# A retention and gated-FFN kernel on one core: the seven-product px stage gets one attention excursion, loads in halves and a later store; the last block another order of loads

## The chip, the cores and the metric

The kernel runs on one core of one Trainium2 chip. The metric is the device time of one execution in microseconds (us); less is better. The kernel before takes 1502.32 us, the median of three runs (1500.96 to 1503.14).

## The reference

Three stages, all in float32. Retention over 8 sequences of 576 tokens with 8 heads of 64, then two feed-forward stages on the 4608 x 512 result:

```python
scores = scale * np.matmul(q, k.transpose(0, 1, 3, 2))
ret = scores * Dmat[None, :, :, :]          # gamma ** (i - j), causal
x = np.matmul(ret, v)                       # -> 4608 x 512
h = (x @ w1) * (x @ w2) @ w3                # 1024 wide
x2 = h @ w_out                              # 512 wide
h2 = x2 @ w_in
g = h2 * np.clip(h2 + 3.0, 0.0, 6.0) / 6.0  # 2048 wide
out = g @ w_out2
```

## The kernel before, in words

Every float32 matrix product is made from two fp32r parts of each operand, high and low, as three matmuls (high x low, high x high, low x high): the helper `mm3` at lines 130 to 132. Casting the high part is ScalarE's (ACT) work, subtracting it to get the low part VectorE's (DVE; the helper at line 135). The engine names in the rows are PE (TensorE), DVE, ACT, POOL (GpSimd) and SP (SyncE, which here only issues loads).

The weights w3 and w_out are multiplied into one 1024 x 512 matrix first (`Wps`, line 513), kept as `Wh` and `Wl` and written to DRAM as `wsd` by `w_quads`. From then on the 4608 tokens go through nine blocks (j = 0 to 8) of 512 tokens. A block (`ffn1`) has two parts:

- 64 steps of x @ w1 and x @ w2 (`f_a`, `f_b`). Each f gives a bank `pa`, copied out by ACT (line 644), and a bank `pb`, multiplied with it on DVE. Four PSUM banks are used in turn.
- px, the product with the joined matrix, 32 steps. In blocks 0 and 8 it is done whole (`mm3`). In blocks 1 to 7 it is `px_str`: a Strassen-Winograd scheme of seven products of quarter size, 24 matmuls of 128x256 each (line 771, 168 in a px). Each product streams an operand of 1 MB (`wb` from `wsd`, `load_w`, line 728) into one of three buffers. Operands 0 and 1 are loaded during the first part, operand 2 when px starts; operand i + 3 goes into the buffer of operand i when product i has ended. Products use banks A, C, B, D, A, D, C: the sixth product adds to bank D, after DVE has read the fourth out of it (line 746, `x<-px`), and the seventh to bank C.

The order of the work is written out by hand: `at(s, f)` puts a piece of work into step s, and every `mm3` and some matmuls of px call `tick`, which emits what stands in that step. `B0 + SPB * n` is the first step of block n, with SPB = 96; `E0` is the first step of block 8. Each engine and each DMA queue then runs its own instructions in the order in which they were emitted, so a wait at the head of one holds up all that is behind it. SP, which has no other work, issues loads as soon as their own waits allow, however early that is in steps.

Between the matmuls stand four attention excursions a block (`excursion`, table `ex`): small matmuls for one tile of 128 tokens (lines 214, 251), after which DVE makes P, S and x (lines 228, 247, 289) and loads of `kv` and `qk` two tiles ahead are issued from POOL (lines 198, 193). `v_scale` (line 204) scales a loaded kv tile on DVE.

Also between them, the weights of the second feed-forward are prepared, one "i" job (w_in) and one "q" job (w_out2) a block (`job`): two raw loads of 512 KB (`wr`), `weights` on ACT (lines 155, 156) and DVE (160, 164), sums (859), high part (862), low part (135), and a store of 1.75 MB (870), all through one staging buffer `stg`/`stghi`. Four `w_job`s do the same for the joined matrix in block 0 and 1 (`wj`, lines 592 to 606).

In block 8, `w_again` loads `Wl` and `Wh` back, `load_xop` and `load_set` load the operands of the second feed-forward (`xop`, `wset`).

Of the kernel before, what the change touches and what calls it, by code (L numbers as in the profile page):

```python
# [7 lines left out]
F32 = mybir.dt.float32  # L8
# [19 lines left out]
def retention_moe_kernel(  # L28
# [20 lines left out]
    nc = tc.nc  # L49
# [15 lines left out]
    TPB = BLK1 // 128  # L65
# [7 lines left out]
    NSET = M2 // 2  # L73
# [44 lines left out]
    def at(s, f):  # L118
        slots.setdefault(max(s, now[0]), []).append(f)
# [200 lines left out]
    with tc.manual_schedule():  # L320
# [38 lines left out]
        B0 = LEAD + 8 * KF  # L359
# [112 lines left out]

        ex = {-1: LEAD + 35, 0: LEAD + 40, 1: LEAD + 45, 2: LEAD + 50, 3: LEAD + 55, 4: B0 + 53, 5: B0 + 63, 6: B0 + 74, 7: B0 + 85}
        for t in range(2 * TPB, NTI):
            ex[t] = B0 + SPB * (t // TPB - 1) + (24, 45, 68, 85)[t % TPB]
        for t in range(-1, NTI):
            at(ex[t], lambda t=t: excursion(t))
            if t >= 0:
                if t == TPB - 1:
                    at(ex[t] + 1, lambda t=t: x_out(t))  # L480
                if t + 1 < NTI:
                    at(ex[t] + 1, lambda t=t: (p_mask(t + 1), s_add(t + 1)))
                if t < 3:
                    at(ex[t] + 1, lambda t=t: v_scale(t + 2))
                if t != TPB - 1:
                    at(ex[t] + 1, lambda t=t: x_out(t))
                at(ex[t] + 2, lambda t=t: x_hi(t))
                at(ex[t] + (3 if t < 2 * TPB else 4), lambda t=t: x_lo(t))
                for i in ([4] if t == 1 else [t + 2] if 2 < t < NTI - 2 else []):
                    at(ex[t] + 1, lambda i=i: load_kv(i))  # L490
                for i in ([t + 3] if t + 3 < 2 * TPB else [t + 2] if 2 * TPB <= t + 2 < NTI else []):
                    at(ex[t] + 1, lambda i=i: load_qk(i))
            if 2 < t < NTI - 2:
                at(B0 + 30 if t == 3 else ex[t + 1] - (4 if t < 7 else 5), lambda t=t: v_scale(t + 2))
        at(LEAD + 33, lambda: v_scale(0))
        at(ex[-1] + 1, lambda: (p_mask(0), s_add(0)))
        at(LEAD + 37, lambda: v_scale(1))
# [76 lines left out]
        def w_again(low):  # L574
            if low:
                lo = [Wp.tile([128, n, DM], F32R, tag=t, name=t) for t, n in (("Wl", 5), ("Wm", 3))]
                whole[1] = lambda f: lo[0][:, f] if f < 5 else lo[1][:, f - 5]
            else:
                h = Wp.tile([128, KF, DM], F32R, tag="Wh", name="Wh")
                whole[0] = lambda f: h[:, f]  # L580
            for o, (c, k) in enumerate(quads):
                src = wsd[o].rearrange("k p h n -> p h k n")
                for to, x in ([(h[:, k:k + 4], src[:, 0])] if not low else [(lo[0][:, 0:4], src[:, 1])] if not k else [(lo[0][:, 4:5], src[:, 1, 0:1]), (lo[1], src[:, 1, 1:4])]):
                    nc.gpsimd.dma_start(out=to[:, :, c:c + 256].bitcast(F32), in_=x)

        def w_job(q, s):
            def sums():
# [21 lines left out]
                at(s + d, f)  # L609

        at(B0 + 44, w_quads)
        for q, d in enumerate((65, 73, 81, 92)):
            w_job(q, B0 + d)
        at(B0 + SPB + 1, open_a)
        at(B0 + SPB + 6, open_st)
# [107 lines left out]
        WORD = (0, 4, 5, 6, 1, 3, 7)  # L723
        w_at = {}

        def load_w(i, b):
            w_at[i] = t = st["wb"][:, b] if b < 2 else st["w3"]
            nc.sync.dma_start(out=t.rearrange("p k h n -> p k (h n)").bitcast(F32), in_=wsd[WORD[i]].rearrange("k p h n -> p k (h n)"))

        def px_str(j):  # L730
            e = j % 2
            rt = x_ps[e].tile([128, 4, BLK1], F32, tag="xh", name="x1")
            st["w3"] = x_ps[e].tile([128, 4, 2, 256], F32R, tag="xl", name="wb")
            a, c, b, d = turn
            bank = {k: mm_bank("px", i) for k, i in (("A", a), ("C", c), ("B", b), ("D", d))}
            turn[:] = [a, b, d, c]
            pair, keep = st["pair"], st["keep"]
            load_w(2, 2)

            def two(k):  # L740
                return bank[k].rearrange("p (m n) -> p m n", m=2)

            U, C11, V, W = (rt[:, 0:2, 0:256], rt[:, 0:2, 256:512], rt[:, 2:4, 0:256], rt[:, 2:4, 256:512])

            def add(out_ap, x, y):
                nc.vector.tensor_tensor(out=out_ap, in0=x, in1=y, op=ALU.add)

            def parts(q):
                at(now[0] + q, lambda: nc.scalar.copy(out=pair[q][:, 0, 0:2], in_=keep[q]))
                at(now[0] + q + 2, lambda: sub(nc.vector, pair[q][:, 1, 0:2], keep[q], pair[q][:, 0, 0:2]))  # L750

            after = (lambda: nc.scalar.copy(out=V, in_=two("A")),
                     lambda: [parts(q) for q in range(4)],
                     lambda: add(U, V, two("B")),
                     lambda: (add(W, U, two("D")), add(V, W, two("C"))),
                     lambda: nc.scalar.copy(out=C11, in_=two("A")),
                     lambda: add(W, U, two("D")),
                     lambda: add(U, U, two("C")))
            seen = set()
            for i, (k, o) in enumerate((("A", 0), ("C", 1), ("B", 3), ("D", 4), ("A", 2), ("D", 1), ("C", 0))):  # L760
                w = w_at.pop(i)
                for kk in range(4):
                    for m in range(2):
                        n = 8 * i + 2 * kk + m
                        if 4 * n % 7 < 4:
                            tick()
                        ms = slice(128 * m, 128 * m + 128)
                        out_ap = bank[k][:, 256 * m:256 * m + 256]
                        hi, lo = pair[kk][:, 0, o], pair[kk][:, 1, o]
                        for x, y in ((0, hi), (0, lo), (1, hi)):  # L770
                            nc.tensor.matmul(out=out_ap, lhsT=w[:, kk, x, ms], rhs=y, start=k not in seen, stop=kk == 3 and x == 1, skip_group_check=True)  # L771
                            seen.add(k)
                if i + 3 < 7:
                    load_w(i + 3, (e, 1 - e, 2)[i % 3])
                if i == 1:
                    after[1]()
                else:
                    at(now[0], after[i])
            xs = x_ps[e].tile([128, 2, 4, 256], F32, tag="xl", name="xs")
            hl = [st["wb"][:, i].rearrange("p k h n -> p (k h) n") for i in range(2)]  # L780
            for m, s in enumerate((now[0], now[0] + 14)):
                b1, b2, d = rt[:, m], rt[:, 2 + m], xs[:, m]
                b11, b12, b21, b22 = b1[:, 0:HB1], b1[:, HB1:BLK1], b2[:, 0:HB1], b2[:, HB1:BLK1]
                parts_ = ((0, 2, b2.rearrange("p (o n) -> p o n", o=2)), (6, 7, b1[:, 0:HB1].rearrange("p (o n) -> p o n", o=1)), (2, 6, d))

                def sums(d=d, v=(b11, b12, b21, b22)):
                    for o, a, b in ((0, v[1], v[0]), (1, v[3], d[:, 0]), (2, v[3], v[1]), (3, v[2], d[:, 1])):
                        sub(nc.vector, d[:, o], a, b)

                def hi(parts_=parts_):  # L790
                    for a, b, t in parts_:
                        nc.scalar.copy(out=hl[0][:, a:b], in_=t)

                def lo(parts_=parts_):
                    for a, b, t in parts_:
                        sub(nc.vector, hl[1][:, a:b], t, hl[0][:, a:b])

                def store(m=m):
                    sb = next(i for i, (b0, n) in enumerate(SBS) if b0 <= j < b0 + n)
                    a = HB1 * (j - SBS[sb][0])  # L800
                    for h, t in enumerate(hl):
                        nc.scalar.dma_start(out=xod[sb][:, :, m, h, a:a + HB1].rearrange("o p n -> p o n"), in_=t[:, 0:7].bitcast(F32))

                for x, f in ((1, sums), (2, hi), (3, lo), (6, store)):
                    at(s + x, f)
# [47 lines left out]
        def job(key, srcs, sums_of, outs, s):  # L853
# [15 lines left out]
                    o = outs(hl)  # L869
                    nc.scalar.dma_start(out=o, in_=t if len(o.shape) == 2 else t.rearrange("p (o n) -> p o n", o=7))  # L870

            for d, f in ((10, sums), (11, hi), (14, lo), (19, store)):
                at(s + d, f)

        A_SUMS = ((4, 0, 1, ALU.add), (5, 4, 2, ALU.subtract), (6, 2, 0, ALU.subtract), (7, 3, 5, ALU.subtract))
        B_SUMS = ((4, 0, 1, ALU.subtract), (5, 2, 4, ALU.subtract), (6, 2, 0, ALU.subtract), (7, 3, 5, ALU.subtract))
        for n in range(NSET):
            job(("i", n), (w_in2[n + NSET], w_in2[n]), A_SUMS, lambda hl, n=n: wid[n, hl], B0 + SPB * n + SPB + (20 if n < NSET - 1 else 24))
            job(("q", n), (w_out2[n], w_out2[n + NSET]), B_SUMS,
                lambda hl, n=n: wqd[:, :, n, hl].rearrange("o p n -> p o n"), B0 + SPB * n + SPB + (46 if n < NSET - 1 else 48))  # L880

        wset, xop = {}, {}
        SETS = (0, 1, 2, 3, 4, 5, 6, 7)
# [48 lines left out]
            signs[:] = [xo_p.tile([128, 4 * BLK1], I32, tag="xl", name="raw")[:, 1024:1536]]  # L932
            nc.gpsimd.memset(signs[0], 0)

        at(E0 + 23, late_sign)
        at(E0 + 14, open_late)
        for i, s in enumerate((24, 58, 26, 28, 32, 38, 104)):
            at(E0 + s, lambda i=i: load_xop(0, i))
        WTAGS = ("A1", "B1", "A2", "B2")
        for n, (t, s) in enumerate((("A1", 62), ("B1", 70), ("A2", 80), ("s4", 105), ("s5", 107), ("B2", 112), ("s6", 119), ("s7", 133))):  # L940
# [434 lines left out]
```

## Time and profile before

| | us |
|---|---|
| median of three runs | 1502.32 |
| the profiled execution | 1500.72 |
| its span, first to last instruction | 1499.0 |
| PE busy | 1434.6 (96% of the span) |
| DVE busy | 1091.4 (73%) |
| ACT busy | 572.0 (38%) |
| granted TensorE clock, mean | 0.981 |

The profiled execution lies 1.6 us under the median of the runs; 1.7 us of it lie around the span. PE is the engine that is nearly always busy, so what a change is worth is looked for in the few places where PE waits, and in the stretches where its granted clock is under 1.00 (full speed, 2.4 GHz; 0.50 is 1.2 GHz). A busy PE at half clock is busy for twice as long.

### The profile page before, as it was taken

To read this page: it belongs to the slowest core of one execution; us is meant where nothing else is said; L and a number is where in the kernel's file an instruction comes from. 1 tells how busy PE (TensorE), PEld (TensorE's weight loads), DVE (VectorE), ACT (ScalarE), POOL (GpSimd) and SP (SyncE) were. 2 spreads that over 40 slices of the span, in tenths; PEclk is the share of its full clock that TensorE was granted. 3 is DMA by queue.
4 is the path that set the end of the run, shared out by engine and by line. 5 is a ranking of instruction groups with operands and counts; after the bars stand their busy time and mean duration, and the time that the engine had idled before them with its cause. 6 is when DMAs were issued, how large, how long until landed. Compare 5 with 4: busy or idle time off the path is not lost.

```text
span 1499.0 us, 27907 instructions
## 1 busy us (share of the span) xinstructions
PE 1434.6 (96%) x11315; PEld 1217.8 (81%) x11315; DVE 1091.4 (73%) x1880; ACT 572.0 (38%) x842; POOL 150.1 (10%) x339
## 2 busy tenths in 40 slices
PE   9999889899898989899969999999999999999999
PEld 5588778788787888888857898888888888888888
DVE  7889677858585858586525666666668988988987
ACT  7572333333232424233323343333334333344342
POOL 1101000000000000000101233222221000000000
PEclk9999989999999999999989999999999999999999
DMA  9775776767678678776778975464798444444442
GB/s 364 276 253 175 262 254 238 274 236 273 249 261 292 240 275 288 270 264 246 251 310 312 369 257 196 166 250 165 293 357 304 141 141 141 141 135 132 127 134 65
DMA packets 210801, 351.31 MB, mean 234 GB/s; under 512 B 10384, under 2 KB 139184, under 8 KB 207088
## 3 DMA queue, kind: packets, MB, share of 16 engines
q1 hardware_dynamic: 137392, 208.69, 40.5%
q0 software_dynamic: 22976, 77.91, 14.0%
q10 hardware_dynamic: 50304, 62.92, 12.4%
q8 instruction: 89, 1.46, 0.4%
q14 instruction: 40, 0.33, 0.1%
HBM read 231.51 MB, written 117.96 MB: 233 GB/s over the span
## 4 chain that ended last, share of the span: by engine, by line
PE 86%; DMA 9%; DVE 3%; issue 1%; POOL 0%; ACT 0%; SPq 0%; ACTq 0%; DVEq 0%; POOLq 0%
PE pb L1297 15%; PE pb L130 11%; PE pb L131 11%; PE pb L132 11%; PE pb L1298 8%; PE px L771 8%; DMA wb<-wsd 5%; PE pa L130 4%; PE pa L131 4%; PE pa L132 4%; PE Wps L513 4%; PE z L251 2%; PE sc L214 2%; DMA xop<-xod 1%; DMA wqd<-stg 1%
## 5 line engine op out<-in xcount | busy, mean ns | idle before, releaser
L1297 PE MATMUL pb<-wq,op 128*128 128x512 f32 x1000 | 346.7, 391 | 0.0
L1298 PE MATMUL pb<-wq,op 128*128 128x256 f32 x1000 | 280.0, 280 | 0.0
L1297 PEld LDWEIGHTS pb<-wq,op 128*128 128x128 f32 x1000 | 187.0, 187 | 41.0
L130 PE MATMUL pb<-xop,wset 128*128 128x512 f32 (+1 forms) x558 | 205.9, 369 | 3.1 <-DMA xop<-xod 1.7
L131 PE MATMUL pb<-xop,wset 128*128 128x512 f32 (+1 forms) x558 | 205.3, 368 | 0.0
L132 PE MATMUL pb<-xop,wset 128*128 128x512 f32 (+1 forms) x558 | 205.2, 368 | 0.0
L1175 ACT CAST op<-unit 128x1024 fp32r<-128x1024 f32 x126 | 131.5, 1052 | 174.1 <-DVE unit L1161 146.7
L771 PE MATMUL px<-pair,wb 128*128 128x256 f32 x1176 | 162.0, 301 | 36.6 <-DMA wb<-wsd 35.6
L771 PEld LDWEIGHTS px<-pair,wb 128*128 128x128 f32 x1176 | 157.1, 209 | 39.9 <-issue 36.8
L1298 PEld LDWEIGHTS pb<-wq,op 128*128 128x128 f32 x1000 | 189.0, 189 | 0.0
L135 DVE TENSOR_TENSOR op<-unit,op 128x1024 fp32r<-128x1024 f32 x126 | 154.0, 1223 | 30.9 <-ACT op L1175 30.9
L130 PEld LDWEIGHTS pb<-xop,wset 128*128 128x128 f32 x558 | 105.2, 189 | 22.5 <-issue 2.1
L132 PEld LDWEIGHTS pb<-xop,wset 128*128 128x128 f32 x558 | 105.2, 189 | 17.3
L131 PEld LDWEIGHTS pb<-xop,wset 128*128 128x128 f32 x558 | 105.2, 189 | 17.3
L130 PE MATMUL pb<-xh,w2h 128*128 128x512 f32 x288 | 113.7, 395 | 4.9 <-ACT stg L819 4.9
L131 PE MATMUL pb<-xl,w2h 128*128 128x512 f32 x288 | 112.8, 392 | 0.0
L132 PE MATMUL pb<-xh,w2l 128*128 128x512 f32 x288 | 112.8, 392 | 0.0
L130 PE MATMUL pa<-xh,w1h 128*128 128x512 f32 x280 | 109.8, 392 | 0.0
L131 PE MATMUL pa<-xl,w1h 128*128 128x512 f32 x280 | 109.2, 390 | 0.1
L132 PE MATMUL pa<-xh,w1l 128*128 128x512 f32 x280 | 109.0, 389 | 0.0
L1161 DVE TENSOR_TENSOR unit<-unit 128x1024 f32<-128x1024 f32 x72 | 87.9, 1220 | 0.6
L297 ACT CAST xh<-x 128x512 fp32r<-128x512 f32 x36 | 22.2, 616 | 166.5 <-DVE x L289 166.5
(207 smaller groups left out, 2259.7 us busy)
## 6 DMA issues: line engine op xcount, KB each, us to landing
wb<-wsd SPq DMA_DIRECT2D x49, 1024.0 KB, 9.2
unit<-gd SPq DMA_DIRECT2D x72, 512.0 KB, 5.3
xop<-xod SPq DMA_DIRECT2D x28, 1024.0 KB, 6.1
xod<-wb ACTq DMA_DIRECT2D x28, 896.0 KB, 4.7
qk<-in_qk_dram POOLq DMA_DIRECT2D x36, 512.0 KB, 6.5
kv<-in_kv_dram POOLq DMA_DIRECT2D x32, 512.0 KB, 5.4
gd<-gw POOLq DMA_DIRECT2D x60, 256.0 KB, 3.1
gd<-g POOLq DMA_DIRECT2D x57, 256.0 KB, 4.2
```

The costliest lines, as they stand in the source:

```text
L130: nc.tensor.matmul(out=out_ap, lhsT=sh, rhs=mh, start=first, stop=False, **kw)
L131: nc.tensor.matmul(out=out_ap, lhsT=sh, rhs=ml, start=False, stop=False, **kw)
L132: nc.tensor.matmul(out=out_ap, lhsT=sl, rhs=mh, start=False, stop=last, **kw)
L135: eng.tensor_tensor(out=out_ap, in0=x, in1=y, op=ALU.subtract)
L214: nc.tensor.matmul(out=out_ap, lhsT=lhsT, rhs=rhs, start=True, stop=True, skip_group_check=True)
L251: c["last"] = nc.tensor.matmul(out=out_ap, lhsT=lhsT, rhs=rhs, start=(a, g) not in c["opened"], stop=True, skip_group_check=True)
L513: nc.tensor.matmul(out=ps, lhsT=w3f[:, n // 4 % 8, n % 4 * 128:n % 4 * 128 + 128], rhs=wo[:, j, :], start=j == 0, stop=j == KF - 1)
L771: nc.tensor.matmul(out=out_ap, lhsT=w[:, kk, x, ms], rhs=y, start=k not in seen, stop=kk == 3 and x == 1, skip_group_check=True)
L1161: nc.vector.tensor_tensor(out=f32_unit(o), in0=t[0], in1=t[1], op=f)
L1175: nc.scalar.copy(out=op_tiles(7 * b + p)[0], in_=src())
L1297: nc.tensor.matmul(out=c[k], lhsT=h[:, ts], rhs=w, start=first and kt == 0, stop=False, skip_group_check=True)
L1298: nc.tensor.matmul(out=c[k][:, 0:256], lhsT=l[:, ts], rhs=w[:, 0:256], start=False, stop=kt == 7, skip_group_check=True)
```

## The change

Five edits, all in the hand-written order and in one load helper.

1. The excursions of blocks 1 to 7 stand at steps 24, 39, 54 and 72 of a block, where they stood at 24, 45, 68 and 85. Px is steps 64 to 95, so it holds one excursion in place of two. The kv and qk loads behind the excursion at 72 are issued 19 steps later than the excursion's other work, at step 92.
2. The q job of a block starts at step 70 in place of 46, and its store comes 24 steps after that (step 94) in place of 19 (step 65).
3. `load_w` loads an operand of px in two halves of 512 KB; in px the first half of operand i + 3 is issued when the first half of product i has ended.
4. The third and fourth `w_job` move from steps 81 and 92 of block 0 to 98 and 106, into block 1.
5. In block 8 `w_again` issues from SP in place of POOL, the i job starts at step 12 in place of 24, the q job at 32 in place of 48, and `late_sign`, `open_late` and the first loads of `xop` move by two to ten steps.

```diff
-            ex[t] = B0 + SPB * (t // TPB - 1) + (24, 45, 68, 85)[t % TPB]
+            ex[t] = B0 + SPB * (t // TPB - 1) + (24, 39, 54, 72)[t % TPB]
...
+                late = 19 if t >= 2 * TPB and t % TPB == 3 else 0
-                    at(ex[t] + 1, lambda i=i: load_kv(i))
+                    at(ex[t] + 1 + late, lambda i=i: load_kv(i))
-                    at(ex[t] + 1, lambda i=i: load_qk(i))
+                    at(ex[t] + 1 + late, lambda i=i: load_qk(i))
-                at(B0 + 30 if t == 3 else ex[t + 1] - (4 if t < 7 else 5), lambda t=t: v_scale(t + 2))
+                at(B0 + 30 if t == 3 else ex[t + 1] - 4, lambda t=t: v_scale(t + 2))
...
-                    nc.gpsimd.dma_start(out=to[:, :, c:c + 256].bitcast(F32), in_=x)
+                    nc.sync.dma_start(out=to[:, :, c:c + 256].bitcast(F32), in_=x)
...
-        for q, d in enumerate((65, 73, 81, 92)):
+        for q, d in enumerate((65, 73, 98, 106)):
...
-        def load_w(i, b):
+        def load_w(i, b, halves=(0, 2)):
             w_at[i] = t = st["wb"][:, b] if b < 2 else st["w3"]
-            nc.sync.dma_start(out=t.rearrange("p k h n -> p k (h n)").bitcast(F32), in_=wsd[WORD[i]].rearrange("k p h n -> p k (h n)"))
+            for k in halves:
+                nc.sync.dma_start(out=t[:, k:k + 2].rearrange("p k h n -> p k (h n)").bitcast(F32), in_=wsd[WORD[i], k:k + 2].rearrange("k p h n -> p k (h n)"))
...
-                if i + 3 < 7:
-                    load_w(i + 3, (e, 1 - e, 2)[i % 3])
+                    if kk % 2 and i + 3 < 7:
+                        load_w(i + 3, (e, 1 - e, 2)[i % 3], (kk - 1,))
...
-            for d, f in ((10, sums), (11, hi), (14, lo), (19, store)):
+            for d, f in ((10, sums), (11, hi), (14, lo), (24 if key[0] == "q" and key[1] < NSET - 1 else 19, store)):
...
-            job(("i", n), ... (20 if n < NSET - 1 else 24))
+            job(("i", n), ... (20 if n < NSET - 1 else 12))
-            job(("q", n), ... (46 if n < NSET - 1 else 48))
+            job(("q", n), ... (70 if n < NSET - 1 else 32))
...
-        at(E0 + 23, late_sign)
-        at(E0 + 14, open_late)
-        for i, s in enumerate((24, 58, 26, 28, 32, 38, 104)):
+        at(E0 + 21, late_sign)
+        at(E0 + 24, open_late)
+        for i, s in enumerate((27, 58, 28, 29, 32, 38, 104)):
```

How the instructions stand, at three places.

PE, the px of block 3 and what borders on it; `z` and `sc` are the excursion's matmuls. Before:

```order
L132 MATMUL pb<-xh,w2l 128x512
L771 MATMUL px<-pair,wb 128x256 x21
L251 MATMUL z<-qk,S 64x64 x8
L251 MATMUL z<-P,kv 64x64 x8
L214 MATMUL sc<-qk 64x64 x16
L214 MATMUL sc<-kv 64x64 x16
L251 MATMUL z<-P,kv 64x64 x8
L771 MATMUL px<-pair,wb 128x256 x90
L251 MATMUL z<-qk,S 64x64 x16
L251 MATMUL z<-P,kv 64x64 x8
```

Now:

```order
L132 MATMUL pb<-xh,w2l 128x512
L773 MATMUL px<-pair,wb 128x256 x42
L251 MATMUL z<-qk,S 64x64 x16
L251 MATMUL z<-P,kv 64x64 x8
L214 MATMUL sc<-qk 64x64 x16
L214 MATMUL sc<-kv 64x64 x16
L251 MATMUL z<-P,kv 64x64 x8
L773 MATMUL px<-pair,wb 128x256 x126
```

The only excursion left in px stands behind 42 matmuls, and 126 follow without a break.

DVE, the same px, from the excursion's x (line 289) on. `x<-x,px` (746, now 748) reads a bank of px; 160 and 164 are the q job's weights, `stg<-stg` of line 859 (now 861) its sums, `pair<-keep` px's own operands. Before:

```order
L289 SCALAR_TENSOR_TENSOR x_3945<-z,cw,ut 128x128 x4
L135 TENSOR_TENSOR xl<-x_3945,xh 128x4x128
L135 TENSOR_TENSOR pair<-keep,pair 128x512 x4
L746 TENSOR_TENSOR x_3839<-x_3839,px 128x2x256
L204 TENSOR_TENSOR kv<-kv,rate 128x2x256
L746 TENSOR_TENSOR x_3839<-x_3839,px 128x2x256 x2
```

Now:

```order
L289 SCALAR_TENSOR_TENSOR x_4055<-z,cw,ut 128x128 x4
L160 SCALAR_TENSOR_TENSOR stg<-stg,sign 128x512
L164 SCALAR_TENSOR_TENSOR stg<-wr,stg 128x512
L135 TENSOR_TENSOR pair<-keep,pair 128x512
L135 TENSOR_TENSOR xl<-x_4055,xh 128x4x128
L135 TENSOR_TENSOR pair<-keep,pair 128x512
L160 SCALAR_TENSOR_TENSOR stg<-stg,sign 128x512
L164 SCALAR_TENSOR_TENSOR stg<-wr,stg 128x512
L135 TENSOR_TENSOR pair<-keep,pair 128x512 x2
L748 TENSOR_TENSOR x_3914<-x_3914,px 128x2x256
L861 TENSOR_TENSOR stg<-stg 128x256 x4
L748 TENSOR_TENSOR x_3914<-x_3914,px 128x2x256 x2
```

The q job's four weight operations and its sums now stand ahead of the second and third reading of px's banks.

SP, the loads from the end of block 7's px into block 8. Before:

```order
L728 DMA wb<-wsd 128x4x512 x5
L107 DMA wr<-in_w_in_dram 128x512 x2
L923 DMA xop<-xod_66 128x2048 x4
L107 DMA wr<-in_w_out_dram 128x512
L923 DMA xop<-xod_66 128x2048
L107 DMA wr<-in_w_out_dram 128x512
L923 DMA xop<-xod_66 128x2048
```

Now:

```order
L730 DMA wb<-wsd 128x2x512 x10
L107 DMA wr<-in_w_in_dram 128x512
L585 DMA Wl<-wsd 128x4x256
L585 DMA Wl<-wsd 128x256
L585 DMA Wm<-wsd 128x3x256
L585 DMA Wl<-wsd 128x4x256
L585 DMA Wl<-wsd 128x256
L585 DMA Wm<-wsd 128x3x256
L107 DMA wr<-in_w_in_dram 128x512
L107 DMA wr<-in_w_out_dram 128x512 x2
L585 DMA Wh<-wsd 128x4x256 x4
L925 DMA xop<-xod_66 128x2048 x6
```

The q job's two raw loads stand ahead of all `xop` loads; the `Wl` loads stand ahead of the i job's second raw load.

## Rows read from the trace of the kernel before

**Rows 1.** Waits of PE, whole span: who waited for what, us in total, times, longest.

```profile
PE px L771 <- DMA wb<-wsd: 35.6, 10, 6.4
PE px L130 <- ACT a L644: 13.7, 1, 13.7
PE pb L130 <- ACT stg L819: 4.9, 1, 4.9
```

**Rows 2.** Timeline of PE, px of block 3: start, length, work, [idle before <-releaser].

```profile
381.26 7.39 PE L771 MATMUL px<-pair,wb 128*128 128x256 f32 x39 [4.99 <-DMA wb<-wsd]
...
390.61 7.10 PE L771 MATMUL px<-pair,wb 128*128 128x256 f32 x57
```

**Rows 3.** Stretches around block 3's wait: us, busy (instructions) per engine, PEclk, DMA share, GB/s.

```profile
376.00:379.00 3.00, 0.27 (x3) 0.07 (x1) 2.45 (x5) 0.20 (x1) 0.00 (x0) 1.00 1.03 407
...
381.30:385.00 3.70, 3.70 (x17) 3.70 (x18) 0.00 (x0) 0.00 (x0) 0.00 (x0) 0.50 0.89 334
```

**Rows 4.** DMA issues, 355 to 402 us: KB each, median us to landing; then qk, 160 to 700.

```profile
wb<-wsd SPq DMA_DIRECT2D x5, 1024.0 KB, 10.1
kv<-in_kv_dram POOLq DMA_DIRECT2D x2, 512.0 KB, 7.5
...
wqd<-stg ACTq DMA_DIRECT2D x1, 896.0 KB, 14.0
...
DMA to landing us min/median/max: 4.6/6.8/10.2
```

**Rows 5.** Timeline of PE, px of blocks 1, 2 and 7.

```profile
220.33 7.62 PE L771 MATMUL px<-pair,wb 128*128 128x256 f32 x39 [6.38 <-DMA wb<-wsd]
...
294.25 3.11 PE L771 MATMUL px<-pair,wb 128*128 128x256 f32 x24 [1.46 <-DMA wb<-wsd]
...
699.76 6.39 PE L771 MATMUL px<-pair,wb 128*128 128x256 f32 x39 [3.11 <-DMA wb<-wsd]
```

**Rows 6.** Timeline of ACT: the end of block 0's px, and block 8's q job.

```profile
160.77 0.59 ACT L819 COPY stg<-px 128x512 f32<-128x512 f32 x1 [8.70 <-DMA xod<-stg]
...
766.58 0.66 ACT L155 ACTIVATE stg<-wr 128x512 f32<-128x512 f32 x1 [21.14 <-DMA wr<-in_w_out_dram]
```

**Rows 7.** DMA issues, 714 to 760 us (block 8).

```profile
wid<-stg ACTq DMA_DIRECT2D x1, 896.0 KB, 7.9
```

**Rows 8.** Timeline of PE, block 3's first part: an excursion, then a step.

```profile
349.44 0.69 PE L251 MATMUL z<-qk,S 64*64 64x64 f32 x32
...
351.46 0.50 PE L130 MATMUL pb<-xh,w2h 128*128 128x512 f32 x1
351.80 0.39 PE L131 MATMUL pb<-xl,w2h 128*128 128x512 f32 x1
352.03 0.40 PE L132 MATMUL pb<-xh,w2l 128*128 128x512 f32 x1
```

**Rows 9.** Timeline of DVE, block 3, 349 to 378 us.

```profile
351.60 0.69 DVE L228 TENSOR_TENSOR P<-sc,mask 128x512 f32<-128x512 f32 x1 [2.60 <-PE z L251]
...
360.06 0.69 DVE L164 SCALAR_TENSOR_TENSOR stg<-wr,stg 128x512 int32<-128x512 int32 x1
360.79 1.55 DVE L859 TENSOR_TENSOR stg<-stg 128x256 f32<-128x256 f32 x4
...
370.95 0.69 DVE L228 TENSOR_TENSOR P<-sc,mask 128x512 f32<-128x512 f32 x1
371.56 0.87 DVE L247 TENSOR_TENSOR S<-S,sc 128x256 f32<-128x256 f32 x2
372.34 1.12 DVE L289 SCALAR_TENSOR_TENSOR x<-z,cw,ut 128x128 f32<-128x128 f32 x4
...
374.76 2.49 DVE L135 TENSOR_TENSOR pair<-keep,pair 128x512 fp32r<-128x512 f32 x4
377.17 0.68 DVE L746 TENSOR_TENSOR x<-x,px 128x512 f32<-128x512 f32 x1
```

**Rows 10.** Timeline of POOL, the same excursion's loads.

```profile
352.72 0.58 POOL L193 DMA_DIRECT2D qk<-in_qk_dram  x1
```

More of the change, by code (lines that the diff above doesn't have):

```diff
@@ L877, in retention_moe_kernel @@
         for n in range(NSET):
-            job(("i", n), (w_in2[n + NSET], w_in2[n]), A_SUMS, lambda hl, n=n: wid[n, hl], B0 + SPB * n + SPB + (20 if n < NSET - 1 else 24))
+            job(("i", n), (w_in2[n + NSET], w_in2[n]), A_SUMS, lambda hl, n=n: wid[n, hl], B0 + SPB * n + SPB + (20 if n < NSET - 1 else 12))
             job(("q", n), (w_out2[n], w_out2[n + NSET]), B_SUMS,
-                lambda hl, n=n: wqd[:, :, n, hl].rearrange("o p n -> p o n"), B0 + SPB * n + SPB + (46 if n < NSET - 1 else 48))
+                lambda hl, n=n: wqd[:, :, n, hl].rearrange("o p n -> p o n"), B0 + SPB * n + SPB + (70 if n < NSET - 1 else 32))
         wset, xop = {}, {}
```

## The prediction

> **What bounds the kernel now.** I read the table of PE's waits first, because PE is busy for 96% of the span and only its waits can be removed by an order of loads. Nearly all of it is three entries: px waits for its streamed operand `wb` for 35.6 us in ten pieces, one wait of 13.7 us stands in block 8, one of 4.9 us at the end of block 0 [rows 1]. Then the timeline of PE in one px, to see what a wait looks like. In block 3 the fourth product starts 4.99 us late and its 39 matmuls take 7.39 us, where 57 matmuls at the end of the same px take 7.10 us, 0.125 each [rows 2]. The reader is to see two losses there, the wait and a slow stretch after it. Third the table of stretches: during the wait DMA runs at 407 GB/s with all 16 engines busy, and after it the granted clock is 0.50, that is 1.2 GHz [rows 3]. Last the DMA issues: an operand of 1 MB takes 10.1 us to land, and a store of the q job and the kv loads are under way at the same time [rows 4]. Operand i + 3 is issued when product i ends and due when product i + 2 ends, two products or 48 x 0.125 = 6.0 us later. So px is bound by transfers that share the DMA engines with others which have no haste.
>
> **What it removes.** *Waits for operands.* With the store at px's end and the kv and qk loads behind it, px's stretch holds only operands 2 to 6, 5 MB, and late in it the next raw loads. Five MB at 407 GB/s [rows 3] take 12.9 us of 168 x 0.125 = 21 us. With halves, each half is issued at the end of half a product and due 2.5 products later, 7.5 us. A transfer of 512 KB landed after 7.5 us in the crowded stretch, the quickest of the qk loads after 4.6 [rows 4]; px without store and kv loads is nearer to the second, so I take the wait as gone: **-35.6 us**. Block 7, whose px has the store but one excursion without loads behind it, still waited 3.11 us [rows 5]; that is the upper bound of what could stay if the store were still there.
>
> *The slow stretch.* The piece of 39 matmuls after the wait lasts 7.62 us in block 1 and 6.39 us in block 7 [rows 5]; the seven of them sum to 48.0 us. At 0.125 each they would take 34.0. **-14.0 us**.
>
> *End of block 0.* ACT's copy out of px waits 8.70 us for the store of `stg` [rows 6], and PE 4.9 us for that copy [rows 1]. The store was queued behind two pieces of the third `w_job` on DVE and ACT; both move behind it, into block 1, where four banks in turn give ACT some 12 steps or 8 us before PE runs dry. The half clock after the wait is priced as the shortest one above, 6.39 - 4.86 = 1.5. **-6.4 us**.
>
> *Block 8.* ACT waits 21.14 us for a raw load of the q job [rows 6], issued late because SP stood at the `xop` loads ahead of it; PE ran out of copied banks and waited 13.7 us [rows 1], plus some 2 us at half clock after it, as in px. Now these raw loads stand ahead. But the q job at step 32 writes the staging buffer which the i job's store, emitted in step 31, still reads. That store lands in 7.9 us [rows 7], 11.6 steps of 0.68 us (three matmuls of 0.23, 351.80 to 352.03 [rows 8]). The i job itself will be some 4 us late, as its second raw load is queued behind 2 MB of `Wl`. So ACT is free at about step 31 + 6 + 11.6 = 49, and with two ops of the q job ahead, its next copy comes at about step 51; PE needs that bank at step 48. That is 2 us of wait, and 2 for what may follow at half clock. Bounds: none, or the old 15.7. **-15.7 + 4 = -11.7 us**.
>
> **What it adds.** *A wait on DVE in px.* Count from the start of px. PE makes 42 matmuls (5.2 us), the excursion (2.0 us, from 349.44 to 351.46 [rows 8]), then 78 more up to the sixth product, which is due at 5.2 + 2.0 + 9.7 = 16.9 us. It adds to bank D and so needs DVE's second `x<-px`, which reads that bank. DVE starts the excursion's P 2.16 us after the excursion's first matmul (351.60 against 349.44 [rows 8, 9]), at 7.4. Then come, in the new order, P 0.69, S 0.87, x 1.12, the weights twice 0.69 (both ops have the shape of the one in the rows), `pair` 2.49 and `xl` 0.69 (P's shape), the second weights 1.38, `x<-px` 0.68, the sums 1.55 and `x<-px` 0.68 [rows 9]: 11.5 us. Starts lie about 0.07 us ahead of the former's end (371.56 against 370.95 + 0.69), nine times, so 10.9. DVE reaches the end at 18.3 us, 1.4 us after PE wants the bank. Before, the wait for operands hid this. Bounds: 0, if overlaps are larger, and 3, if ACT's casts for `pair` and the weights don't keep up. **+1.4 x 7 = +9.8 us**.
>
> *Edits at nothing.* The excursions themselves take the same 2 us wherever they stand. DVE's and ACT's work for the moved ones is covered by PE's matmuls of the first part, where DVE is lighter by the q job; without that cover it would be P, S, x and `xl`, 3.4 us a block [rows 9]. The excursion at 39 leaves its qk load 15 steps and the excursion's 2.1 us: 12.3 us, and 0.75 more to the first use. The POOL issue comes 3.3 us in (352.72 against 349.44 [rows 8, 10]), so 9.8 us are left, against a landing of 6.8 median and 10.2 at most [rows 4]; I take it as in time. The extra issues of halves are SP's, which waits there anyway.
>
> **The sum.** -35.6 - 14.0 - 6.4 - 11.7 + 9.8 = -57.9 us against this execution's own 1500.7: 1442.8. The runs' median lies 1.6 us higher, which gives 1444.4; I say **1445**.
>
> **Halves.** In the crowded stretch half the bytes (kv) took 7.5 us and all of them 10.1 [rows 4]: a half does not land in half the time, though two halves overlap. The Trainium skill, in "DMA: Bandwidth & Descriptors", section "Rules for kernel authors", asks for at least 1 MiB a DMA for full bandwidth, which speaks against this edit. Its fit in the section "Anatomy of one DMA" (2.0 us plus the bytes at 436 GB/s) makes 3.2 us of a half, an estimate; were halves strictly one after the other, an operand would take 6.4 us in place of 4.4, still under the 7.5 us that it has, and the sum would stay.
>
> **The rivals.**
> - *No wait on DVE.* The 1.4 us is a difference of two long sums. If it is nothing, 1445 - 9.8 = **1435**.
> - *The transfers are late all the same*, because a half needs more than the 7.5 us it has. For: the kv row is just at that limit, and DMA stood at 407 GB/s. Against: what crowded it has moved. Priced as block 7, 3.1 + 1.5 us [rows 5], in place of the DVE wait: 1445 - 9.8 + 32 = **1467**.
> - *Short waits cost clock too.* A wait of 1.46 us in block 2 was followed by 24 matmuls in 3.11 us, full pace [rows 5], so I count none. If each of the seven DVE waits cost 2 us of half clock: **1459**. "TensorE: Matmul & The Clock Gate" of the Trainium skill, section "A second HAM failure mode: psum-queue depth-cycling", tells of a kernel whose short idles between groups sent the clock back and forth; block 2's row is against it here.
> - *Block 8 waits as long as before*, since the i job's store lands later among `Wh` and `xop` loads; at 17 us it would: 1445 + 11.7 = **1457**.
> - *Slower: the excursions wait for qk.* The loads behind the excursions at 24 and 39 now have 9.8 us to land. If they land in 14 us, as the q job's store did in the crowd [rows 4], PE waits 4.2 us and loses 2 of clock at two excursions a block: 14 x 6.2 = 87, **1532**. It decides from 9.8 us; from about 12 us on (2.2 + 2 us each) the gain is used up. For: wb, raw loads and the i store stand in that stretch. Against: the largest landing of qk was 10.2.
>
> **How the numbers follow.** Chances: the forecast 0.54, no DVE wait 0.13, late transfers 0.10, clock 0.08, block 8 0.10, slower 0.05. The forecast's own range, from DVE waits of 0.6 to 2.4 us, is 1438 to 1452. The range is 1431 to 1466: it takes in all but late transfers and the slower case, 0.15. A measurement of this kernel tells from no change what is over 0.2%, 3 us. All cases but the last are faster; of the last I leave 0.01 for within 0.2%.
>
> **What would show it.** In the profile after: the wait of px for `wb` gone or under 3 us in total; a new wait of PE in px on DVE's `x<-px` of about 1.4 us, seven times, at the sixth product; a clock of 1.00 through px; no wait for ACT's `stg` copy at block 0; in block 8 a wait of 0 to 5 us on ACT's `a`. Wrong would be: px still waiting for `wb`, `sc` or `z` waiting for qk, or a DVE wait over 3 us.

## The result and the profile after

The changed kernel takes **1451.42 us**, the median of three runs (1450.67 to 1453.22), against 1502.32 before: a ratio of 0.9665, 95% interval 0.9643 to 0.9687. Its profiled execution took 1451.42 with a span of 1449.6. The forecast of 1445 was 6.4 too low, and the time lies inside its range.

PE's waits after the change, whole span (who waited for what, us in total, times, longest), to be read beside [rows 1]:

```profile
PE pa L130 <- ACT a L645: 8.0, 1, 8.0
PE sc L214 <- DVE kv L204: 7.3, 1, 7.3
PE px L773 <- DVE x L748: 4.8, 3, 1.9
PE px L773 <- DMA wb<-wsd: 2.7, 2, 1.6
PE zero L504 <- POOL Wh L502: 2.1, 1, 2.1
PE px L773 <- issue: 1.3, 1, 1.3
```

The 35.6 us for `wb` have become 2.7. Block 8's wait has gone from 13.7 to 8.0, the wait on ACT's `stg` is gone, and two waits are new: px on DVE's `x`, as forecast, and 7.3 us of `sc` on DVE's `kv`, which was not.

PE in px of block 3, its timeline (start, length, work, idle before), beside [rows 2]; the excursion stands between the first two:

```profile
355.43 5.19 PE L773 MATMUL px<-pair,wb 128*128 128x256 f32 x42
...
362.58 9.64 PE L773 MATMUL px<-pair,wb 128*128 128x256 f32 x78
373.65 5.98 PE L773 MATMUL px<-pair,wb 128*128 128x256 f32 x48 [1.43 <-DVE x L748]
```

All 168 matmuls run at 0.125 us each, and the one break is where the sixth product waits for DVE.

Waits alone don't show where the time went. I cut the span at three points that both kernels have: the first matmul of px in block 1, the last of px in block 7, and the first of the last stage (lines 1299 and 1300). A 2.0 us excursion has crossed the first cut, from px of block 1 to the part ahead of it; the last two columns have it put back.

| stretch | before, us | after, us | measured | predicted |
|---|---|---|---|---|
| start to first px matmul of block 1 | 202.9 | 207.0 | +2.1 | -6.4 |
| px of block 1 to px of block 7 | 511.6 | 469.2 | -40.4 | -39.8 |
| block 8 and what follows, to the last stage | 431.3 | 420.5 | -10.8 | -11.7 |
| last stage | 353.2 | 352.9 | -0.3 | 0 |
| sum | 1499.0 | 1449.6 | -49.4 | -57.9 |

The first row is 8.5 us worse than forecast, which is the whole shortfall; what the other rows are off by cancels.

**The end of block 0.** DVE's timeline there, after the change:

```profile
167.21 1.23 DVE L135 TENSOR_TENSOR wj<-wj 128x1024 fp32r<-128x1024 f32 x1 [4.25 <-DMA wsd<-wj]
...
171.54 0.68 DVE L204 TENSOR_TENSOR kv<-kv,rate 128x512 f32<-128x512 f32 x1
```

The third and fourth `w_job` share one buffer and stand eight steps apart. The fourth's low part waits 4.25 us for the third's store, and behind it in DVE's queue stands the scale of a kv tile. The excursion in block 1 needs that tile, so PE waits 7.3 us for it. The granted clock, too, is no longer full afterwards (stretches: us, busy and instructions of PE, PEld, DVE, ACT, POOL, PEclk, DMA share, GB/s):

```profile
172.00:176.00 4.00, 3.72 (x53) 3.19 (x54) 3.90 (x9) 2.27 (x4) 1.28 (x2) 0.50 0.38 129
176.00:180.00 4.00, 4.00 (x16) 3.23 (x15) 3.93 (x10) 1.21 (x2) 0.00 (x0) 0.84 0.99 366
```

**Block 8.** ACT's timeline, beside [rows 6]:

```profile
690.33 0.66 ACT L155 ACTIVATE stg<-wr 128x512 f32<-128x512 f32 x1 [4.96 <-DMA wr<-in_w_in_dram]
...
703.46 0.34 ACTq L872 DMA_DIRECT2D wid<-stg  x1
712.66 0.66 ACT L155 ACTIVATE stg<-wr 128x512 f32<-128x512 f32 x1 [10.29 <-DMA wid<-stg]
716.52 0.56 ACT L645 COPY a<-pa 128x512 f32<-128x512 f32 x1
```

As forecast, the i job's raw load is some 4 us late behind `Wl` (4.96), and the q job's first weight op waits for the i job's store. That store takes 9.2 us to land, not 7.9 [rows 7], and the copy PE wants comes 3.9 us after it.

**The late loads.** POOL's timeline in block 3, beside [rows 10]:

```profile
361.64 0.09 POOL L273 MEMSET token<- 128x1 f32 x1 [11.31 <-PE z L251]
363.14 0.71 POOL L198 DMA_DIRECT2D kv<-in_kv_dram  x1 [1.41 <-PE z L251]
363.84 0.58 POOL L193 DMA_DIRECT2D qk<-in_qk_dram  x1
```

The kv and qk loads emitted 19 steps later are issued 2.6 and 3.3 us after the excursion's first matmul (360.55); before, qk was issued 3.3 us after it as well [rows 8, 10]. In this timeline POOL has nothing else to do or to wait for in between, so a later step is not a later time. No run undoes these 19 steps alone. What the introduction says of these loads ("issued 19 steps later") holds for the steps alone.

### The profile page after: what moved, and what is told of

It reads as the page before. It is cut to its first block, busy times and chain, and to the rows that moved or that the text cites. A ratio compares the mean times of both kernels' runs of the same rounds, so it can differ in the third digit from the quotient of the medians.

```text
span 1449.6 us, 28030 instructions
## 1 busy us (share of the span) xinstructions
PE 1419.8 (98%) x11315; PEld 1204.7 (83%) x11315; DVE 1091.0 (75%) x1880; ACT 573.4 (40%) x842; POOL 143.1 (10%) x329
## 3 DMA queue, kind: packets, MB, share of 16 engines
q0 software_dynamic: 21792, 73.72, 13.7%
## 4 chain that ended last, share of the span: by engine, by line
PE 88%; DVE 6%; DMA 4%; ACT 1%; issue 1%; POOL 0%; ACTq 0%; DVEq 0%; POOLq 0%
PE pb L1299 16%; PE pb L130 12%; PE pb L132 12%; PE pb L131 12%; PE pb L1300 8%; PE px L773 6%; PE pa L130 4%; PE pa L131 4%; PE Wps L514 4%; PE pa L132 4%; PE z L251 2%; PE sc L214 2%; DMA wb<-wsd 1%; DMA xod<-wb 1%; DVE stg L135 1%; DVE pair L135 1%
## 5 line engine op out<-in xcount | busy, mean ns | idle before, releaser
L773 PE MATMUL px<-pair,wb 128*128 128x256 f32 x1176 | 147.6, 286 | 9.0 <-DVE x L748 4.8
L773 PEld LDWEIGHTS px<-pair,wb 128*128 128x128 f32 x1176 | 144.4, 193 | 11.6 <-issue 7.3
L684 ACT CAST pair<-sraw 128x512 fp32r<-128x512 f32 (+1 forms) x56 | 40.8, 728 | 95.6 <-DVE sraw L135 95.6
```

The lines of the kernel that those rows point to most:

```text
L684: nc.scalar.copy(out=st["pair"][f % 4][:, 0, a:b], in_=st["raw"][:, a + 1:b + 1])
```

## The experiments

For each kernel the profile was cut at the same three points (spans in us; first px is the start to the first px matmul). The kernels ran on five chips, on which the kernel before took 1499.17 to 1502.32 us; each ratio is to the kernel before on the same chip, and a difference of 3 us between the medians of two rows tells nothing.

| kernel | runs, median us | ratio to before, 95% interval | first px | px 1 to 7 | block 8 etc. | last stage |
|---|---|---|---|---|---|---|
| before | 1502.32 | | 202.9 | 511.6 | 431.3 | 353.2 |
| after | 1451.42 | 0.9643 to 0.9687 | 207.0 | 469.2 | 420.5 | 352.9 |
| store alone | 1476.97 | 0.9805 to 0.9887 | 203.0 | 485.5 | 434.0 | 353.1 |
| excursions back | 1461.47 | 0.9719 to 0.9763 | 203.4 | 478.6 | 423.9 | 355.9 |
| store back | 1472.91 | 0.9801 to 0.9840 | 207.2 | 488.1 | 421.4 | 353.0 |
| whole loads | 1467.61 | 0.9765 to 0.9819 | 206.6 | 483.0 | 420.1 | 353.0 |
| w_jobs back | 1454.63 | 0.9666 to 0.9737 | 208.5 | 467.6 | 420.3 | 352.9 |
| block 8 back | 1464.21 | 0.9733 to 0.9796 | 207.0 | 470.3 | 436.1 | 353.0 |
| sums later | 1447.05 | 0.9610 to 0.9676 | 206.3 | 468.4 | 420.6 | 352.9 |
| third w_job earlier | 1449.00 | 0.9628 to 0.9685 | 198.1 | 469.9 | 420.9 | 358.9 |
| block 8's q job later | 1447.43 | 0.9631 to 0.9679 | 206.5 | 469.6 | 416.5 | 352.9 |
| loads really late | 1452.62 | 0.9664 to 0.9711 | 206.5 | 469.1 | 422.8 | 353.1 |
| sums and loads later | 1445.72 | 0.9603 to 0.9667 | 206.5 | 459.8 | 421.9 | 356.5 |
| four edits together | 1433.44 | 0.9542 to 0.9579 | 198.5 | 459.6 | 416.9 | 356.5 |

### Each edit undone in the changed kernel

**Excursions back** at 24, 45, 68, 85, and with them the steps of their loads and of `v_scale` as before (not in the lines shown).

```diff
-            ex[t] = B0 + SPB * (t // TPB - 1) + (24, 39, 54, 72)[t % TPB]
+            ex[t] = B0 + SPB * (t // TPB - 1) + (24, 45, 68, 85)[t % TPB]
```

> The changed kernel with the excursions and their loads back at 24, 45, 68, 85. If the q job's store was what crowded px (theory): 7 MB then run in px without the store, under the 10 MB that DMA can move in 25 us, so waits for wb stay under 1.5 us a block and partly hide the DVE wait: 1450 to 1460 us. If the excursions' kv and qk loads crowd it as much as the store (rival): 3 us of wait and 1.5 of clock a block, 1475 to 1485 us.

The median is 10 us over the change's. Px takes 9.4 us more, 2.0 of it the excursion that comes back into it. PE waits for `wb` 6.5 us in six pieces, 3.8 more than after. The time lies just above the theory's range and far from the rival's.

**Store back** at 19 steps, the q job at 46.

```diff
-            for d, f in ((10, sums), (11, hi), (14, lo), (24 if ... else 19, store)):
+            for d, f in ((10, sums), (11, hi), (14, lo), (19, store)):
-                ... B0 + SPB * n + SPB + (70 if n < NSET - 1 else 32))
+                ... B0 + SPB * n + SPB + (46 if n < NSET - 1 else 32))
```

> The changed kernel with the q job back at step 46 and its store at 65, at px's start. Theory (the store crowds px): as block 7 before, 3.1 us of wait and 1.5 of clock a block, while the 0.7 us a block of DVE wait go: about 1478 us. Rival (halves and fewer excursion loads are enough): under 1455 us, or faster than the changed kernel by the DVE waits, 1446 us.

The median is 21.5 us over the change's, 18.9 of it in px. PE's waits:

```profile
PE px L773 <- DMA wb<-wsd: 18.9, 14, 2.7
```

The issues from 355 to 382 us (px of block 3: KB each, median us to landing) say why:

```profile
wb<-wsd SPq DMA_DIRECT2D x10, 512.0 KB, 9.9
...
wqd<-stg ACTq DMA_DIRECT2D x1, 896.0 KB, 15.8
```

In the changed kernel the same ten halves land in 5.7:

```profile
wb<-wsd SPq DMA_DIRECT2D x10, 512.0 KB, 5.7
```

The store in px nearly doubles the landing of the operands: 9.9 us is over the 7.5 they have, 5.7 under it. These are medians of one block; in block 2 (281 to 306 us) they are 10.6 and 6.9. The edit moves the whole q job, its raw loads and its work on DVE and ACT as well; that the store is the cause is read from these landings. The theory holds, with 21.5 us in place of its 27.

**Store alone**: the kernel before with edit 2 and nothing else (the diff is the change's own part 2).

> The kernel before with the second edit alone: q jobs of blocks 1 to 7 at step 70, store at 94. Theory (the store is the larger part of the crowd): px waits for wb fall from 35.6 us to 5 to 15, the clock loss with them; DVE waits of 1 to 3 us a block may come, since two excursions and the q job now share px: 1465 to 1480 us. Rival (the three edits only work together): over 1490 us.

It is 23 us faster than the kernel before on that chip (1499.57), in the theory's range; px still waits 16.4 us for `wb`, a little over the 5 to 15 expected. So the later q job, with its store, is the largest single part, and it gives about as much alone (23) as it costs to undo (21.5).

**Whole loads**: `load_w` issues 1 MB at the end of a product.

```diff
-            for k in halves:
-                nc.sync.dma_start(out=t[:, k:k + 2]..., in_=wsd[WORD[i], k:k + 2]...)
+            nc.sync.dma_start(out=t..., in_=wsd[WORD[i]]...)
```

> The changed kernel with operands of px loaded whole, 1 MB, when a product has ended. Theory (halves buy 1.5 us of time for a load that lands in about 8 us and has 6): waits of 1 to 3 us a block, of which the DVE wait hides one: 1455 to 1465 us. Rival (a whole load is served as fast as two halves, and the room is enough): within 3 us of 1451, with px waits for wb unchanged near 3 us in total.

The median is 16 us over the change's, 13.8 in px; the theory's direction, beyond its range. Its waits and its issues from 355 to 382 us:

```profile
PE px L772 <- DMA wb<-wsd: 18.9, 6, 3.6
```

```profile
wb<-wsd SPq DMA_DIRECT2D x5, 1024.0 KB, 9.0
```

A half lands in 5.7 us against 9.0, which is not half the time, but it has 7.5 us from issue to use where the whole operand has 6.0. At 9.0 the operand misses that by 3.0, and the six waits of 3.2 us in the mean come close to that. "DMA: Bandwidth & Descriptors" of the Trainium skill, section "Rules for kernel authors", asks for 1 MiB a DMA for bandwidth; this run does not measure bandwidth, but shows a case in which 512 KB is faster, since a transfer's start and its due time are what counts. No half landed in the 3.2 us that the prediction estimated: the 98 halves of the changed kernel took 3.6 to 9.7.

**Third and fourth w_job back** at 81 and 92.

```diff
-        for q, d in enumerate((65, 73, 98, 106)):
+        for q, d in enumerate((65, 73, 81, 92)):
```

> The changed kernel with the third and fourth w_job back at steps 81 and 92 of block 0. Theory (the 7.3 us that PE waits for the kv scale in block 1 come from the fourth w_job, on which DVE stands in front of the scale until the third's store has landed): that wait and some 2.5 us at half clock go, the 4.9 us wait for ACT's stg copy and 1.5 us of clock come back: about 1448 us. Rival (the kv load itself was late): the wait of 7 us stays beside the old one, 1458 us.

The median is 3 us over the change's, with overlapping intervals, and the profiles are 0.3 apart in span. The waits show the exchange:

```profile
PE pb L130 <- ACT stg L821: 6.3, 1, 6.3
```

The wait for `kv` falls to 1.9, and the one for `stg` is back with 6.3. Edit 4 swapped one wait for another of its size; by the first cut (208.5 against 207.0) it gained 1.5 us. The theory was right on the mechanism, and its 1448 was not reached.

**Block 8 back** (edit 5 undone: `w_again` on POOL, i job at 24, q job at 48, `late_sign`, `open_late` and the `xop` loads as before).

> The changed kernel with block 8 as before. Theory: 13.7 us of wait and 2 of clock in place of 8.0 and 1.5: about 1458 us. Rival (what block 8 waits is set by DMA as a whole, so that it only moves): within 3 us of 1451.

The median is 13 us over the change's; in the profile block 8 takes 436.1 against 420.5. PE waits 17.0 us there:

```profile
PE px L130 <- ACT a L645: 17.0, 1, 17.0
```

So the rival is out. The loss is about twice the theory's 7 us: the wait is longer than the 13.7 us of before, and why stays open.

### What is left, taken away

**Sums later**: the q job's sums, high and low parts 4 steps later, so that they stand behind the reading of the bank that the sixth product wants.

```diff
-            for d, f in ((10, sums), (11, hi), (14, lo), ...
+            z = 4 if key[0] == "q" and key[1] < NSET - 1 else 0
+            for d, f in ((10 + z, sums), (11 + z, hi), (14 + z, lo), ...
```

> The changed kernel with the q job's sums, high and low part 4 steps later, behind DVE's reading of bank D and C. Theory (PE's wait at the sixth product is DVE's queue): the waits of 4.8 us for x<-px and 1.3 us with no releaser go: 1445 to 1447 us. Rival (the operand is no earlier than DVE was): waits for wb take their place, 1450 to 1452 us.

No wait on DVE is left, but others stand in its place:

```profile
PE px L773 <- DMA wb<-wsd: 8.6, 6, 2.4
```

Five of the six stand ahead of the second half of the fifth product, 12 matmuls ahead of the sixth. PE reaches that point no earlier than in the changed kernel; the half lands later: in block 1 PE gets it 17.7 us after px's start and not 16.4. Profiles of kernels whose px is the changed kernel's own differ as much (waits for `wb` of 1.4 us with the w_jobs back, 8.1 with block 8 back). So the rival's waits came, but this profile alone doesn't show that the DVE wait had hidden them. Px is 0.8 us shorter; the median is at the theory's upper edge, 4 us under the change's with overlapping intervals.

**Loads really late**: kv and qk of the excursion at 72 are issued from SP, behind px's operands.

```diff
-        nc.gpsimd.dma_start(out=x..., in_=qk...)
+        (nc.sync if late else nc.gpsimd).dma_start(out=x..., in_=qk...)
```

(and the same for kv.)

> The kv and qk loads that the change meant to issue 19 steps later are put on SP, behind px's operands, so that they do land later. Theory: the operand waits in px of blocks 1 and 2 (1.6 and 1.1 us) come from these loads' traffic and go; but PE then reaches the sixth product before the sums on DVE are through, as in blocks 3 to 6, and waits there some 1.4 us for DVE instead: 1449 to 1452, no difference. Rival: the operand waits have another cause (the i job's raw loads, the halves' own latency) and stay: the same time, but with wb waits in the list. Other rival: the next block's first excursion now waits for its kv or qk: over 1455.

No operand wait is left, and the median is that of the change: 1452.62. PE's waits:

```profile
PE px L773 <- issue: 9.2, 6, 2.0
```

"Issue" is a wait without a named releaser, here six breaks of 1.5 us in the mean, each ahead of the sixth product. They are the wait on DVE: in block 3 the second reading of px's banks is the first of the two operations in the row below, done at 372.88, and PE starts the sixth product at 372.96.

```profile
372.18 1.40 DVE L748 TENSOR_TENSOR x<-x,px 128x512 f32<-128x512 f32 x2
```

The theory holds, with a time just above its 1449 to 1452: without these loads behind the excursion the operands land in time, and the wait on DVE takes the place of the wait for them.

**Sums and loads later**, both edits.

> Both at once: kv and qk behind px's operands, and the q job's sums, hi and lo 4 steps later. Theory: with the sums alone moved, 6 operand waits of 2.4 us in the mean (8.6 us in all) took the place of the waits on DVE; if they come from the traffic of kv and qk, they go here, and px runs without a wait of over 1 us: about 1447 - 6 = 1441. Rival: the operands are late by themselves (each is asked for three products ahead, and that is the limit): the waits stay near 8 us and the time near 1447.

```profile
PE px L773 <- issue: 1.4, 5, 0.7
```

Px of blocks 1 to 7 takes 459.8 us against 469.2: 9.4 us, about the 8.8 us of waits that px had. Each edit alone gave at most 0.8. PE is held at two places 12 matmuls (1.5 us) apart, and each hides the other: after the change, in block 2, it gets the operand 17.0 us after px's start and so is at the sixth product at 18.5, while DVE, in block 3, is through at 18.2. The median, 1445.72, is 5.7 lower and not the 10 expected, and the intervals overlap. In the profiled execution the last stage took 356.5 against 352.9 (see below) and block 8 1.4 more.

**Third w_job earlier**, at 88 in place of 98.

```diff
-        for q, d in enumerate((65, 73, 98, 106)):
+        for q, d in enumerate((65, 73, 88, 106)):
```

> The changed kernel with the third w_job at step 88 of block 0 in place of 98, the fourth at 106 as now. Theory: the third's store has landed when the fourth wants its buffer, so neither the 7.3 us wait for the kv scale nor the old 4.9 us wait is there: about 1442 us. Rival (any w_job in the end of block 0 delays the store of stg): the old wait of 5 us and its clock come back, about 1448 us.

```profile
PE sc L214 <- DVE kv L204: 0.7, 1, 0.7
```

The wait for `kv` is gone without one for `stg`, and px of block 1 starts 8.9 us earlier (198.1). DVE waits for no store of a `w_job` there any more. That settles the cause in block 0: the two jobs' shared buffer. The median is only 2.4 us lower, with overlapping intervals; in the profile the last stage gives 6.0 us back.

**Block 8's q job later**, at 46, its raw loads where they were.

```diff
+            early = 14 if key == ("q", NSET - 1) else 0
-            weights((key, 0), s - 12, s, ...
+            weights((key, 0), s - 12 - early, s, ...
-                ... (70 if n < NSET - 1 else 32))
+                ... (70 if n < NSET - 1 else 46))
```

> The q job of block 8 goes from step 32 to step 46, its two raw loads stay at steps 20 and 24. Theory: block 8's wait of 8.0 us is the chain wid store (landing 9.2 us) - weight op of the q job on ACT - copy of a, because the q job's weight op stands on ACT ahead of the copy; with the job behind the copy the wait and the 1.5 us of half clock after it go: 1451.4 - 9.5 = about 1442. Rival: the copy of a then waits for something else that comes at about the same time (the raw load, the sign, a weight set), the wait stays over 5 us or turns up a few us later at a pb or px matmul: 1447 or more.

The wait of 8.0 us is gone, and the stretch is 4.0 us shorter, not 9.5. ACT's timeline at the block's end:

```profile
744.18 0.59 ACT L821 COPY stg<-px 128x512 f32<-128x512 f32 x1 [12.88 <-DMA wqd<-stg]
```

The q job's store, now later, takes 19.85 us to land among the `xop` loads (the chain of waits has it from 724.25 to 744.18), and the copy of px stands behind it. The first products of the next stage then wait:

```profile
PE pb L130 <- DMA xop<-xod: 2.7, 1, 2.7
```

With 0.9 and 0.7 us for ACT beside it this is 4.3 us. The rival was right.

**Four edits together.**

> All four edits together: the third w_job at step 88 of block 0, the q jobs' sums, hi and lo 4 steps later, kv and qk of the excursion at 72 on SP behind px's operands, block 8's q job at step 46. Theory: the profiles show the gains apart, so they add: the kv wait of 7.3 us and its half clock (px of block 1 started 8.9 us earlier with the w_job moved), px's waits of 8.8 us, and 4 us net of block 8's wait: 1451.4 - 8.9 - 8.8 - 4.0 = about 1430. Rival: the last stage runs at 285 instead of 290 instructions per 50 us, as it did in the profiles of the kernels with the w_job moved and, from 1285 us on, with the sums and loads moved; then some 6 us are given back: about 1436.

1433.44 us (1430.48 to 1435.09), a ratio of 0.9542 to 0.9579, clear of the change's 0.9643 to 0.9687. Its profile has no wait of PE over 2.1 us, and a mean granted clock of 1.00. The three cuts show 8.5, 9.6 and 3.6 us gained, and the last stage 3.6 us lost: between theory and rival.

## Why the prediction was right, point by point

- **Waits for operands, -35.6.** Right but for 2.7 us in blocks 1 and 2. That they stayed under the 3 us of the forecast's sign is the luck of one execution: with the same px, other profiles show up to 8.1 (above). Px is hardly longer for it (470.3 against 469.2), as the wait on DVE shrinks. One reason given was wrong: "px's stretch holds only operands 2 to 6, 5 MB". The kv and qk loads are not behind the store but in px, with the i job's raw loads later, and "loads really late" shows that the waits that stayed come from them. The store was what mattered, as "store back" shows, and halves were needed as well ("whole loads": 18.9 us of waits).
- **The slow stretch, -14.0.** Right. With the operand waits down by 32.9 us and 5.2 of DVE and issue waits added, 12.7 of the -40.4 are left for clock. In block 6 a wait of 1.95 us did cost clock: the 48 matmuls behind it took 7.47 us where those of block 3 took 5.98 (below).
- **A wait on DVE in px, +9.8.** The right place and nearly the right size, where it came: 1.43 us in block 3, and 1.45, 1.26 (under "issue") and 1.95 in blocks 4 to 6. DVE's order was as counted, and in block 3 PE had the bank 18.2 us after px's start, where the forecast said 18.3:

```profile
362.71 0.69 DVE L228 TENSOR_TENSOR P<-sc,mask 128x512 f32<-128x512 f32 x1 [3.13 <-PE z L251]
...
370.81 0.68 DVE L748 TENSOR_TENSOR x<-x,px 128x512 f32<-128x512 f32 x1
371.40 1.55 DVE L861 TENSOR_TENSOR stg<-stg 128x256 f32<-128x256 f32 x4
372.87 1.40 DVE L748 TENSOR_TENSOR x<-x,px 128x512 f32<-128x512 f32 x2
```

  In blocks 1 and 2 an operand wait of 1.1 and 1.6 us took its place, and block 7 had none: four times 1.5, 6.1 us in all, not seven times 1.4. (The lower end of the forecast's own range, from waits of 0.6 us, is 1439 by its sum, not 1438.)
- **End of block 0, -6.4.** The step that failed: it came out at +2.1. The term followed ACT's copy and its four banks. It did not ask what stands on DVE behind the moved `w_job`s, nor what the fourth waits for: the third's store reads the same buffer and stands at step 104, five steps ahead of the fourth's low part. "Third w_job earlier" shows it: at 88 the cut falls from 207.0 to 198.1. With the excursion that crossed the cut put back, that is 6.8 us under before, so the price of 6.4 was right and what it left out was the buffer.
- **Block 8, -11.7.** The sum was right (-10.8), its parts not. The wait was sized at 2 us plus 2 of clock; it was 8.0 and 1.4 (3.88 us at a clock of 0.63), since the store was issued about 40 steps of 0.68 us into the block (703.46 against 676.34) and not 37, landed in 9.2 us, and the copy came 3.9 us later and not two steps (1.4). The mechanism, ACT held by the i job's store, was the predicted one. That the term balanced is luck: 3.1 us of waits at the next stage's start, which the term did not count (`xop`, `stg` and `stghi` in the list of before, shown here), went as well; with them -6.3 (15.7 to 9.4) becomes -9.4, and 1.4 us of the -10.8 stay unassigned:

```profile
PE pb L130 <- DMA xop<-xod: 1.7, 1, 1.7
...
PE pb L130 <- DVE stg L974: 0.8, 1, 0.8
PE pb L130 <- ACT stghi L1036: 0.6, 1, 0.6
```

- **Edits at nothing.** Right: no wait of `sc` or `z` on qk in any block, so the slower case did not come.

## What to carry to other kernels

When a job is moved to free one engine, list what stands behind it on every engine that it uses, and what its buffer's last reader is: here ACT was freed and DVE blocked. A transfer that must arrive in time is won by an earlier start and by taking unhurried stores off its stretch, more than by size. Where two waits end at nearly the same time, removing one shows nothing; take both away before calling either harmless.

## What the runs showed of the hardware that was not expected

**The last stage runs at two paces at the same granted clock.** One window of it, in the changed kernel:

```profile
1300.00:1350.00 50.00, 50.00 (x290) 44.07 (x289) 45.15 (x60) 20.59 (x24) 0.00 (x0) 1.00 0.39 112
```

The same window with the third w_job earlier:

```profile
1300.00:1350.00 50.00, 50.00 (x285) 43.36 (x284) 43.93 (x60) 20.13 (x23) 0.00 (x0) 1.00 0.46 130
```

PE is never idle and the clock reads 1.00 in both, yet 285 matmuls pass in place of 290. Over the stage that is 6.0 us. In three other profiles (excursions back, sums and loads later, four edits together) the pace fell only in the course of the stage, between about 1240 and 1300 us, and cost 3.0 to 3.6. No edit is in all four kernels, and that stage was not touched. The DMA share is not what sets it: from 1350 to 1400 us the changed kernel has a share of 0.56 and keeps 290. Why the pace falls stays open; it means that a few us of an earlier gain can be hidden in a median.

**Which wait costs clock.** In px of the changed kernel the clock was 1.00 after waits of 1.43 us (block 3) and 1.64 (block 2). In block 6, after 1.95 us, it was not:

```profile
298.00:302.00 4.00, 3.93 (x32) 3.94 (x33) 3.53 (x5) 2.17 (x2) 0.00 (x0) 1.00 1.05 407
...
374.00:378.00 4.00, 4.00 (x36) 4.00 (x35) 2.99 (x3) 1.64 (x3) 0.00 (x0) 1.00 1.04 400
596.00:600.00 4.00, 3.52 (x19) 3.55 (x20) 3.09 (x3) 1.99 (x2) 0.00 (x0) 0.64 1.04 399
```

The length alone doesn't decide it. With the w_jobs back the same place in block 6 had a wait of 1.96 us, and the clock stayed at 1.00. In "whole loads" a wait of 3.04 us (block 2) was followed by a slow stretch (clock 0.62 from 300 to 304 us), and a longer one, 3.14 us in block 4, was not (1.00 from 455 to 459):

```profile
300.14 10.13 PE L772 MATMUL px<-pair,wb 128*128 128x256 f32 x72 [3.04 <-DMA wb<-wsd]
...
454.93 8.87 PE L772 MATMUL px<-pair,wb 128*128 128x256 f32 x72 [3.14 <-DMA wb<-wsd]
```

What decides it stays open. So the rival "short waits cost clock too" was true of one px wait in six after the change, and of none with the w_jobs back. "TensorE: Matmul & The Clock Gate" of the Trainium skill, section "A second HAM failure mode: psum-queue depth-cycling", tells of a clock that goes back and forth with short idles; the trace of the changed kernel shows it after one of its short waits alone.
